# Clustered attention followed by a gated MLP on one core: routing in one matmul pass, one PV copy per period in batch 0, two items prepared later, centroid roots on GpSimd

## The chip, the core and the metric

The kernel runs on one core of a Trainium2 chip. The core's engines run side by side, each with its own queue of instructions: TensorE (PE; its weight loads are shown as PEld), VectorE (DVE), ScalarE (ACT), GpSimd (POOL) and SyncE (SP), which here only issues DMAs. The metric is the device time of one execution in microseconds (us): the median of several runs.

## What is computed

Inputs: q, k, v of 4 batches x 8 heads x 768 tokens x 64 numbers, 16 centroids per head, and two MLP weight matrices (512 x 2048 and 2048 x 512).

```python
q_n, k_n, c_n = (t / (norm(t, axis=-1) + 1e-6) for t in (q, k, centroids))
q_assign = argmax(einsum('bhsd,hcd->bhsc', q_n, c_n), axis=-1)
k_assign = argmax(einsum('bhsd,hcd->bhsc', k_n, c_n), axis=-1)
scores = q @ k.T / sqrt(64)
scores = where(q_assign == k_assign, scores, -1e9)
attn = softmax(scores) @ v
x = attn, heads side by side              # 3072 x 512
h = x @ w_in
out = (h * sigmoid(h)) @ w_out            # 3072 x 512
```

Each query attends only to the keys with the same nearest centroid; then comes an MLP whose hidden values are multiplied by their own sigmoid.

## The kernel before

**Tiles.** Tokens lie 128 to a tile; a head has 6 query tiles and 6 key tiles. q and k are split into two f16 numbers, hi and lo, so that products of 128 numbers (hi and lo of 64) give nearly f32 results. After the codes have been written over the lo half, a score is a product over 96 rows: 64 of hi and 32 of a one-hot code of the centroid.

**Items.** The routing of queries and keys is done in 34 items (line 71). Items 0 to 7 hold the 6 key tiles and the first 3 query tiles of one head of batch 0; items 8 and 9 hold the other query tiles of four heads each; items 10 to 33 hold the 12 tiles of one head of batches 1 to 3. Item n is head n - 2 from there on. For each item, in this order:

1. `load_qk` (105): DMAs on SP into a `qk` buffer (4 of them).
2. `hi` (136, ACT) and `lo` (142, DVE): the split into `hl` (3 buffers).
3. Transpose: for items 0 to 7 `pe_tr` (154, PE, into PSUM) and `tr_out` (164, copies by ACT and DVE); for items 8 to 33 `xpose` (147), a transposing DMA issued by SP into an `ab` buffer (5).
4. `logits` (174): per tile two matmuls with 16 columns, accumulated in PSUM: the tile against `stk` (the centroids' high part, twice) and against `ckl` (their low part). The sum lies in `psL`, in a PSUM buffer of the group "mm" (2 buffers) up to item 11, then of the group "pv" (1 buffer).
5. `am_max` (189, DVE): the maximum over 16 columns, read from `psL`, then a one-hot mask (`is_ge`), read from `psL` too.
6. `am_back` (197) and `codes` (204), both on DVE: the mask is transposed in 32 x 32 blocks and written in four copies of 32 rows into the item's tile.

**Attention.** The kernel issues its work in steps T (lines 536 to 564); six steps are one period p, which is one head for batches 1 to 3 (p = 8 to 31). In batch 0 a period is half of two heads: three query tiles of heads 2(p % 4) and 2(p % 4) + 1. In step T stand, in this order: the scores of step T + 1 (`qk_mm`, 215; two PSUM buffers "st"), then logits, PE transposes and `x_tr` if they are due, a part of the MLP (`pop_mlp`), `pv_mm` if due, the `exp` of step T on ACT, from T = 48 on `am_max`, the MLP's pending activations of the step before, `evac` if due, and then whatever else is due in T in the order in which it was listed.

`pv_mm` (251) multiplies the weights P with v and a column of ones, so that the last of 65 columns is the softmax's denominator; the result is `pO`, in the one PSUM buffer of the group "pv". `evac` (267, DVE) takes the reciprocal of that column and multiplies, into `xp`. In batch 0 a period has two such pairs, c = 0 and 1, one per head: `pv_mm` in steps 6p + 4 and 6p + 7, `evac` one step after each, three blocks of 64 columns at a time. From batch 1 on there is one `evac` of six blocks per period. In batch 0 and for the last two heads `x_tr` (281, PE, into "mm") transposes `xp`, and `x_out` (288, ACT) copies it to `xt`, the MLP's input; for the other heads a transposing DMA does it (`x_dma`, 296).

**MLP.** `unit_a` (309) is four matmuls of 384 columns into `ph` ("mm", 2 buffers), then tanh on ACT (320) and one operation on DVE (321) into `gt`. `unit_b` (329) is four matmuls of 512 columns into `po`, and after four of those a copy (342) and the output DMA. `pop_mlp` (350) issues units at rates fixed by the step. `ready` (510) says in which step the MLP may start on a half batch; what is left after the last step is done in the loop at 572.

**When an item's work is due.** `due(n)` (458) is d, the step in which an item must be routed: 6(n - 2) - 1 for n >= 10. For n >= 10, logits stand at d - 6, `am_max` at d - 5, `am_back` and `codes` at d - 4, `xpose` at d - 23, `lo` at d - 25, `hi` at d - 27, `load_qk` at d - 40. For items 8 and 9 `xpose` stands at d - 11. All of it is written out by hand: nothing is reordered later, and each engine's queue runs strictly in this order.

**The start** (376 to 455). SP loads the centroids, then items 0 to 2, v of head 0 and item 3. PE runs `fill(10)`, ten matmuls on zeros whose result nobody reads. ACT loads its table for square roots, squares and sums the centroids (405) and takes the root (407); DVE refines the root in two rounds of four operations (417 to 428), with `lo(0)` between them; then six operations end in `chl`, the centroids in f16 high and low parts. `fill(4)` (442) stands on PE ahead of the transpose of `chl` (444), and three copies on DVE (446 to 448) write `stk` and `ckl`. Then come `lo(1)`, `logits(0)` and so on.

Of the kernel before, what the change touches and what calls it, by code (L numbers as in the profile page):

```python
# [9 lines left out]
f32 = mybir.dt.float32  # L10
f16 = mybir.dt.float16
AF = mybir.ActivationFunctionType
ALU = mybir.AluOpType
AX = mybir.AxisListType
# [3 lines left out]
def kernel(  # L18
# [10 lines left out]
    nc = tc.nc  # L29
    B, H, S, D = q.shape  # L30
    HC = centroids.shape[1]
# [3 lines left out]
    NJ = S // 128  # L35
# [3 lines left out]
    HALF = S // 2  # L39
# [5 lines left out]
    NSPLIT = H // 2  # L45
# [4 lines left out]
    const = ctx.enter_context(tc.tile_pool(name="const", bufs=1))  # L50
# [4 lines left out]
    wout_s = const.tile([128, NFB, DM], f16, name="wout_s")  # L55
    xts = [[const.tile([128, S], f16, name=f"xt{r}_{n}") for r in range(NR)] for n in range(2)]
    vts = [const.tile([128, NJ, D + 2], f16, name=f"vt{n}") for n in range(H)]
    stk = const.tile([128, H, HC], f16, name="stk")
    ckl = const.tile([128, H, HC], f16, name="ckl")

    ohp = [[const.tile([128, 12, 32], f16, name=f"oh{m}_{n}") for n in range(r)] for m, r in enumerate((2, 1, 2))]
    mxs = const.tile([128, 34, 12], f32, name="mxs")
# [15 lines left out]
    def head_of(p, s):  # L78
        return 2 * (p % NSPLIT) + s if p < H else p
# [18 lines left out]
    def width(n):  # L98
        return 3 * len(items[n])
# [41 lines left out]
    @per_item  # L141
    def lo(n):
        ho, lw, src = parts(n)
        nc.vector.scalar_tensor_tensor(out=lw, in0=src, scalar=QS, in1=ho, op0=ALU.mult, op1=ALU.subtract)  # L144
# [9 lines left out]
    def pe_tr(n):  # L154
        hl = hls[n]
        trs[n] = []
        for a, w in ((0, NJ), (NJ, NJ // 2)):
            tag, bufs = ("po", 1) if a == 0 else ("mm", 2)
            pT = ps.tile([128, w * 128], f16, name="pT", tag=tag, bufs=bufs)
            for t in range(w):  # L160
                nc.tensor.transpose(pT[:, 128 * t : 128 * t + 128], hl[:, a + t].rearrange("p c d -> p (c d)"), ident)
            trs[n].append(pT)
# [7 lines left out]
        abs_[n] = ab  # L170


    @per_item
    def logits(n):
        ab, w = abs_[n], width(n)

        tag, bufs = ("mm", 2) if n < H + 4 else ("pv", 1)
        psL = ps.tile([128, 12, HC], f32, name="psL", tag=tag, bufs=bufs)[:, 0:w]
        for t in range(w):
            for c, st in ((stk, True), (ckl, False)):  # L180
                nc.tensor.matmul(psL[:, t, :], ab[:, t, :], c[:, items[n][t // 3][0] % H, :], start=st, stop=not st)  # L181
        psLs[n] = psL

    def oh_of(n):
# [3 lines left out]
    @per_item  # L188
    def am_max(n):
        psL, w = psLs.pop(n), width(n)  # L190
        mx = mxs[:, n, 0:w]
        nc.vector.tensor_reduce(out=mx, in_=psL, axis=AX.X, op=ALU.max)
        nc.vector.tensor_tensor(
            out=oh_of(n)[:, :, 0:HC], in0=psL, in1=mx.unsqueeze(2).to_broadcast([128, w, HC]), op=ALU.is_ge
        )
# [53 lines left out]


    def pv_mm(p, c, i0, i1):
        hd = head_of(p, c)
        if i0 == 0:
            pOs[p, c] = ps.tile([128, NJ, D + 2], f32, name="pO", tag="pv", bufs=1)
        for i in range(i0, i1):
            for j in range(NJ):
                if p < H:
                    o = (j % 2) * HALF + 128 * i
                    lhsT = Ps[NJ * p + 3 * c + j // 2][:, o : o + 128]
                else:  # L260
                    lhsT = Ps[NJ * p + j][:, 128 * i : 128 * i + 128]
                nc.tensor.matmul(  # L262
                    pOs[p, c][:, i, 0 : D + 1], lhsT, vts[hd % H][:, j, 0 : D + 1], start=(j == 0), stop=(j == NJ - 1)
                )


    def evac(p, c):
        hd, pO = head_of(p, c), pOs.pop((p, c))
        i0, w = (3 * (p // NSPLIT), 3) if p < H else (0, NJ)
        if hd % 2 == 0:  # L270
            xps[hd // 2] = mp.tile([128, NJ, 128], f16, name="xp", bufs=3)
        xp = xps[hd // 2]
        rz = rzs[:, hd, i0 : i0 + w]
        nc.vector.reciprocal(rz, pO[:, 0:w, D])
        nc.vector.tensor_tensor(  # L275
            out=xp[:, 0:w, D * (hd % 2) : D * (hd % 2) + D], in0=pO[:, 0:w, 0:D],
            in1=rz.unsqueeze(2).to_broadcast([128, w, D]), op=ALU.mult,
        )


# [7 lines left out]
    def x_out(hd, a, w):  # L288
        b, r = divmod(hd // 2, NR)
        for i in range(w // 3):  # L290
            o = 128 * a + i * HALF
            nc.scalar.activation(
                out=xts[b % 2][r][:, o : o + HALF], in_=pXs.pop((hd // 2, i)), func=AF.Copy, bias=0.0, scale=1.0
            )

    def x_dma(hd):
        b, r = divmod(hd // 2, NR)
# [59 lines left out]
    def fill(n):  # L357
        if n:
            junk = ps.tile([128, 1024], f32, name="junk", tag="st", bufs=2)[:, 0:512]
            for _ in range(n):  # L360
                nc.tensor.matmul(junk, zz[:, 0:128], zz, start=True, stop=True)  # L361
# [13 lines left out]

    nc.vector.memset(zz, 0.0)
    cw_ = mp.tile([128, D], f32, name="craw")
    nc.sync.dma_start(cw_, centroids.rearrange("h c d -> (h c) d"))
    load_qk(0)
    load_qk(1)  # L380
    load_qk(2)
# [4 lines left out]
    def at(T, f, *a):  # L386
        steps.setdefault(T, []).append((f, a))

    nc.scalar.preload_act_table(AF.Sqrt)
    fill(10)  # L390
    ident = const.tile([128, 128], f16, name="ident")
    make_identity(nc, ident)
# [8 lines left out]
    abks = [g0[:, 1152 * n : 1152 * (n + 1)].rearrange("p (n c) -> p n c", c=128) for n in range(5)]  # L401
    abks += [const.tile([128, 9, 128], f16, name=f"abk{n}") for n in range(5, H)]
    csq = mp.tile([128, D], f32, name="csq")
    cs = mp.tile([128, 1], f32, name="cs")
    nc.scalar.activation(out=csq, in_=cw_, func=AF.Square, bias=0.0, scale=1.0, accum_out=cs)
    cy = mp.tile([128, 1], f32, name="cy", bufs=3)
    nc.scalar.activation(out=cy, in_=cs, func=AF.Sqrt, bias=0.0, scale=1.0)
    hi(0)
    nc.scalar.preload_act_table(AF.Exp)
    for vt in vts:  # L410
        nc.gpsimd.memset(vt[:, :, D : D + 2], 1.0)
    for oh in ohp[1] + ohp[2]:
# [1 line left out]
        nc.gpsimd.memset(oh[:, :, HC : HC + 1], 1.0)  # L414
    for oh in ohp[2]:
        nc.gpsimd.memset(oh[:, 0:NJ, HC : HC + 1], -1.0)
    for i in range(2):
        cr = mp.tile([128, 1], f32, name="cr", bufs=2)
        nc.vector.reciprocal(cr, cy)
        ct = mp.tile([128, 1], f32, name="ct", bufs=2)  # L420
        nc.vector.tensor_tensor(out=ct, in0=cs, in1=cr, op=ALU.mult)
        ct2 = mp.tile([128, 1], f32, name="ct2", bufs=2)
        nc.vector.tensor_tensor(out=ct2, in0=ct, in1=cy, op=ALU.add)
        cy = mp.tile([128, 1], f32, name="cy", bufs=3)
        nc.vector.tensor_scalar(out=cy, in0=ct2, scalar1=0.5, scalar2=None, op0=ALU.mult)
        if i == 0:
            lo(0)
            pe_tr(0)
    cyp = mp.tile([128, 1], f32, name="cyp")
    nc.vector.tensor_scalar(out=cyp, in0=cy, scalar1=1e-6, scalar2=None, op0=ALU.add)  # L430
    cinv = mp.tile([128, 1], f32, name="cinv")
# [7 lines left out]
    )  # L439
    tr_out(0)  # L440
    hi(1)
    fill(4)
    pst1 = ps.tile([128, 128], f16, name="pst1", tag="mm", bufs=2)
    nc.tensor.transpose(pst1, chl.rearrange("p a d -> p (a d)"), ident)
    chv = pst1[0:64, :].rearrange("d (h c) -> d h c", c=HC)
    nc.vector.tensor_copy(stk[0:64], chv)
    nc.vector.tensor_copy(stk[64:128], chv)
    nc.vector.tensor_copy(ckl[0:64], pst1[64:128, :].rearrange("d (h c) -> d h c", c=HC))
    lo(1)
    logits(0)  # L450
    pe_tr(1)
# [13 lines left out]
    for n in range(NI):  # L465
        d = due(n)
        near = n < H + 2
        if n < H:
            if n > 0:
                at(3 * n - 3, am_back, n)  # L470
                at(3 * n - 3, codes, n)
                at(3 * n - 4, am_max, n)
                at(3 * n - 5, logits, n)
            if n > 1:
                at(3 * n - 8, tr_out, n)
                at(3 * n - 9, pe_tr, n)
                at(3 * n - 11, lo, n)
                at(3 * n - 12, hi, n)
        else:
            e = d + 2 if near else d  # L480
            at(e - 4, am_back, n)
            at(e - 4, codes, n)
            at(e - 5, am_max, n)
            at(e - 6, logits, n)
            x = d - (11 if near else 23)
            at(x, xpose, n)
            at(x - 2, lo, n)
            at(x - 4, hi, n)
        if n > 3:
            at(d - (24 if near else 40), load_qk, n)  # L490
    for n in range(NBH):
        hd = n
# [18 lines left out]
    for p in range(NBH):  # L511
        if p < H:
            for c in range(2):
                T = NJ * p + 3 * c + 4
                pv_at[T] = (p, c, 0, 3)
                evac_at[T + 1] = (p, c)
            E = T + 1
            at(E + 1, x_tr, 2 * (p % NSPLIT), 3, "mm")
            at(E + 1, x_out, 2 * (p % NSPLIT), 3 * (p // NSPLIT), 3)
            if p % NSPLIT == NSPLIT - 1:  # L520
                ready[E + 3] = [(0, p // NSPLIT)]
            continue
        T = NJ * (p + 1) + 1
        for i in range(3):
            pv_at[T + i] = (p, 0, 2 * i, 2 * i + 2)
        E = T + 3
        evac_at[E] = (p, 0)
        if p == NBH - 1:
            at(E + 1, x_tr, p - 1, NJ, "mm")
            at(E + 1, x_out, p - 1, 0, NJ)  # L530
        elif p % 2 == 1:
            at(E + 1, x_dma, p - 1)
            if p % H == H - 1:
                ready[E + 8] = [(p // H, 0), (p // H, 1)]
# [76 lines left out]
```

## Time and profile before

| | |
|---|---|
| median of 3 runs | 339.13 us (338.73 to 339.54) |
| the profiled execution | 339.54 us |
| its span in the profile | 337.8 us |
| PE busy | 314.1 us (93%) |
| ACT busy | 235.5 us (70%) |
| DVE busy | 220.0 us (65%) |
| POOL busy | 33.8 us (10%) |
| chain that ended last: PE, DVE, ACT, DMA | 70%, 11%, 7%, 7% |

The profile shows one execution: when each instruction started and ended, and what an idle engine waited for. Matmuls are pipelined: each lasts longer than the distance to the next one's start, so many short ones add up to more busy time than they take of the queue. A group is named by line, engine and tiles (out<-in), with partitions x elements, the count, the busy time, the mean of one, and the idle time ahead of its instructions with who ended it. Batch 0's periods run from about 12 to 84 us, those of batches 1 to 3 until some 270 us, and after that only the MLP is left. The granted clock is the share of full speed at which TensorE's clock ran.

### The profile page before, as it was taken

The page shows a single profiled execution, that of the slowest core. Times are in us where ns is not written, and L with a number is a line of the kernel's source. Part 1 is how long each engine was busy: PE and PEld are TensorE (multiplying, and loading weights), DVE is VectorE, ACT ScalarE, POOL GpSimd, SP SyncE. Part 2 cuts the span into 40 slices and gives each one's busy share as a digit, 9 for nine tenths or more (in the row PEclk, how much of TensorE's full clock was granted, in tenths as well). Part 3 has the DMA queues.
Part 4 walks back from the last instruction along what each step waited for, and adds up shares of the span by engine and source line. Part 5 has one row for each costly group of instructions (what it writes and reads, how often), then busy time and mean ns, then how long its engine had stood idle before and what let it go on. Part 6 is the DMA issues. An engine that isn't in the chain of part 4 may idle for free.

```text
span 337.8 us, 8356 instructions
## 1 busy us (share of the span) xinstructions
PE 314.1 (93%) x3350; PEld 190.8 (57%) x3350; DVE 220.0 (65%) x537; ACT 235.5 (70%) x377; POOL 33.8 (10%) x84
## 2 busy tenths in 40 slices
PE   7787978967999999999998999999999999999995
PEld 3455645644666665566665666666666654555542
DVE  5899774675877768756777777766655442365431
ACT  6797898968988888787788777877778541264310
POOL 3234222130000000100000000000000000000000
PEclk9997999999999999999999999999999999999999
DMA  6799999985577676897296666362301001100121
GB/s 187 191 229 206 221 127 231 177 173 126 123 174 165 167 187 171 151 236 129 99 191 148 120 165 145 88 102 65 79 33 25 31 33 54 73 0 0 37 88 63
DMA packets 71510, 42.32 MB, mean 125 GB/s; under 512 B 52016, under 2 KB 67376, under 8 KB 71472
## 3 DMA queue, kind: packets, MB, share of 16 engines
q1 hardware_dynamic: 68144, 37.60, 47.1%
q0 software_dynamic: 3328, 4.20, 8.0%
q8 instruction: 26, 0.43, 0.5%
q14 instruction: 12, 0.10, 0.1%
HBM read 27.30 MB, written 6.29 MB: 99 GB/s over the span
## 4 chain that ended last, share of the span: by engine, by line
PE 70%; DVE 11%; ACT 7%; DMA 7%; issue 3%; SPq 1%; DVEq 0%; ACTq 0%
PE po L335 23%; PE ph L316 16%; PE pS L231 7%; PE pO L262 7%; PE psL L181 5%; PE sth L316 4%; PE pS L232 4%; DMA qk<-in_q_dram 3%; DVE gt L321 3%; DMA ab<-hl 2%; ACT P L246 2%; ACT tn L320 2%; ACT P L241 2%; PE junk L361 2%; DVE hl L144 2%
## 5 line engine op out<-in xcount | busy, mean ns | idle before, releaser
L246 ACT ACTIVATE P<-pS 128x768 f16<-128x768 f32 x144 | 114.5, 816 | 29.7 <-PE pS L232 28.6
L321 DVE SCALAR_TENSOR_TENSOR gt<-tn,ph 128x384 f16<-128x384 f32 x105 | 58.0, 553 | 58.4 <-ACT tn L320 57.1
L335 PE MATMUL po<-wout_s,gt 128*128 128x512 f16 x384 | 94.3, 379 | 0.0
L316 PE MATMUL ph<-xt,win_s 128*128 128x384 f16 x420 | 84.6, 325 | 2.1 <-DVE gt L321 1.8
L316 PEld LDWEIGHTS <-win_s 128*128 128x128 f16 x512 | 48.4, 97 | 36.4 <-issue 3.1
L320 ACT ACTIVATE tn<-ph 128x384 f32<-128x384 f32 x105 | 52.0, 495 | 16.8 <-PE ph L316 15.6
L335 PEld LDWEIGHTS <-gt 128*128 128x128 f16 x384 | 37.0, 97 | 37.4
L262 PEld LDWEIGHTS <-P 128*128 128x128 f16 x1152 | 47.4, 97 | 14.3 <-DVE xp L275 0.8
L231 PE MATMUL pS<-ab 96*128 96x512 f16 x144 | 54.3, 380 | 1.1 <-ACT P L246 1.1
L262 PE MATMUL pO<-vt,P 128*128 128x65 f16 x1152 | 50.8, 193 | 0.5 <-DVE xp L275 0.4
L241 ACT ACTIVATE P<-pS 128x768 f16<-128x768 f32 x48 | 37.9, 813 | 5.3 <-PE pS L225 5.0
L232 PE MATMUL pS<-ab 96*128 96x256 f16 x144 | 38.9, 270 | 0.0
L127 POOL CAST vt<-vn 128x384 f16<-128x384 f32 x32 | 18.4, 574 | 174.2 <-DMA vn<-in_v_dram 110.5
L144 DVE SCALAR_TENSOR_TENSOR hl<-qk,hl 128x768 f16<-128x768 f32 (+1 forms) x34 | 30.8, 911 | 1.0 <-ACT hl L139 0.8
L320 ACT ACTIVATE tn<-sth 128x384 f32<-128x384 f32 x23 | 11.0, 490 | 27.2 <-PE sth L316 20.1
L207 DVE TENSOR_SCALAR ab<-ohT 32x384 f16<-32x384 f16 x104 | 27.5, 264 | 1.9
L139 ACT ACTIVATE hl<-qk 128x768 f16<-128x768 f32 (+1 forms) x34 | 27.3, 808 | 1.3 <-DMA qk<-in_q_dram 1.3
L342 DVE TENSOR_SCALAR ot<-po 128x512 f32<-128x512 f32 x24 | 16.5, 688 | 17.7 <-PE po L335 17.2
L181 PEld LDWEIGHTS <-ab 128*128 128x128 f16 x624 | 18.7, 96 | 8.6 <-issue 5.3
L321 DVE SCALAR_TENSOR_TENSOR gt<-tn,sth 128x384 f16<-128x384 f32 x23 | 12.5, 553 | 14.1 <-ACT tn L320 14.1
L181 PE MATMUL psL<-stk,ab 128*128 128x16 f16 x312 | 18.8, 169 | 3.0 <-DVE xp L275 1.8
L275 DVE TENSOR_TENSOR xp<-pO,rzs 128x384 f16<-128x384 f32 (+1 forms) x40 | 19.1, 477 | 1.4
(73 smaller groups left out, 248.1 us busy)
## 6 DMA issues: line engine op xcount, KB each, us to landing
qk<-in_k_dram SPq DMA_DIRECT2D x32, 192.0 KB, 3.3
vn<-in_v_dram SPq DMA_DIRECT2D x32, 192.0 KB, 3.3
out_dram<-ot SPq DMA_DIRECT2D x24, 256.0 KB, 2.0
qk<-in_q_dram SPq DMA_DIRECT2D x24, 192.0 KB, 3.1
win_s<-in_moe_w_in_dram POOLq DMA_DIRECT2D x8, 256.0 KB, 6.1
wout_s<-in_moe_w_out_dram POOLq DMA_DIRECT2D x8, 256.0 KB, 6.0
qk<-in_q_dram SPq DMA_DIRECT2D x16, 96.0 KB, 4.0
ab<-hl SPq DMA_TRANSPOSE x26, 3.9
```

The lines of the kernel that those rows point to most:

```text
L144: nc.vector.scalar_tensor_tensor(out=lw, in0=src, scalar=QS, in1=ho, op0=ALU.mult, op1=ALU.subtract)
L181: nc.tensor.matmul(psL[:, t, :], ab[:, t, :], c[:, items[n][t // 3][0] % H, :], start=st, stop=not st)
L207: nc.vector.tensor_scalar(out=ab[64:96, 0:w, 32 * g : 32 * g + 32], in0=ohT[32 * g : 32 * g + 32, :].rearrange("p (t i) -> p t i", i=32), ...
L231: nc.tensor.matmul(pS[:, 0:512], lhsT, q_tiles(p, 0, 4), start=True, stop=True)
L232: nc.tensor.matmul(pS[:, 512:768], lhsT, q_tiles(p, 4, 2), start=True, stop=True)
L241: nc.scalar.activation(out=P.rearrange("p (c x) -> p c x", c=2), in_=pS.rearrange("p (c x) -> p c x", c=2)[:, :, 0:HALF], func=AF.Exp, bia ...
L246: nc.scalar.activation(out=P, in_=pS[:, 0:S], func=AF.Exp, bias=0.0, scale=ESC)
L262: nc.tensor.matmul(pOs[p, c][:, i, 0 : D + 1], lhsT, vts[hd % H][:, j, 0 : D + 1], start=(j == 0), stop=(j == NJ - 1))
L316: nc.tensor.matmul(ph, win_s[:, r, ts(fb, 128)], xts[b % 2][r][:, T0 : T0 + HALF], start=(r == 0), stop=(r == NR - 1))
L320: nc.scalar.activation(out=tn, in_=ph, func=AF.Tanh, bias=0.0, scale=0.5)
L321: nc.vector.scalar_tensor_tensor(out=gt[:, fb, :], in0=tn, scalar=1.0, in1=ph, op0=ALU.add, op1=ALU.mult)
L335: nc.tensor.matmul(po, gt[:, fc, ts(t, 128)], wout_s[:, fc, :], start=(fc == 0), stop=(fc == NFB - 1))
```

## The change

1. **Routing.** `stk` and `ckl` become the two halves of one tile `cst`, 32 columns per head. For items 10 to 33 `logits` issues one matmul of 32 columns per tile instead of two of 16, and `psL` has 32 columns per tile: both parts side by side. `am_max` first sums the two halves with a reduction on DVE into `lg`, in SBUF; maximum and mask read `lg`. Items 0 to 9 stay with two matmuls.
2. **Batch 0's PV.** Both pairs of a period share one `pO` (three blocks each); one `evac` per period, at step 6p + 8, divides all six.
3. **Batch 0's transposed output.** For p >= 4, `x_tr` and `x_out` come two steps after `evac` instead of one, with `ready` following, and `x_out` is a copy on DVE, after the other work listed for that step (`lo` of a later item among it), instead of one on ACT.
4. **Items 10 and 11.** `xpose`, `lo` and `hi` stand at d - 15, d - 17 and d - 19: eight steps later. The DMA of item 12 (step 36) then stands ahead of that of item 11 (step 38) on SP.
5. **The start.** The centroid DMA goes to ACT's queue. ACT loads only the table of exp. Square and sum are two operations on DVE; the root is one operation on GpSimd, a power of 0.5, behind a memset; the two refining rounds are gone. `fill(4)` ahead of the transpose of `chl` becomes `fill(3)` behind it.

The loads (`load_qk`), the rates of the MLP and the work after the last step are the same.

```diff
-    stk = const.tile([128, H, HC], f16, name="stk")
-    ckl = const.tile([128, H, HC], f16, name="ckl")
+    cst = const.tile([128, H, 2 * HC], f16, name="cst")
+    stk, ckl = cst[:, :, 0:HC], cst[:, :, HC : 2 * HC]
...
     def logits(n):
-        psL = ps.tile([128, 12, HC], f32, name="psL", tag=tag, bufs=bufs)[:, 0:w]
+        two = n < H + 2
+        psL = ps.tile([128, 12, HC if two else 2 * HC], f32, name="psL", tag=tag, bufs=bufs)[:, 0:w]
         for t in range(w):
-            for c, st in ((stk, True), (ckl, False)):
-                nc.tensor.matmul(psL[:, t, :], ab[:, t, :], c[:, items[n][t // 3][0] % H, :], start=st, stop=not st)
+            hd = items[n][t // 3][0] % H
+            if two:
+                for c, st in ((stk, True), (ckl, False)):
+                    nc.tensor.matmul(psL[:, t, :], ab[:, t, :], c[:, hd, :], start=st, stop=not st)
+            else:
+                nc.tensor.matmul(psL[:, t, :], ab[:, t, :], cst[:, hd, :], start=True, stop=True)
...
     def am_max(n):
+        if n >= H + 2:
+            lg = mp.tile([128, 12, HC], f32, name="lg", bufs=2)
+            nc.vector.tensor_reduce(out=lg, in_=psL.rearrange("p t (s c) -> p t c s", s=2), axis=AX.X, op=ALU.add)
+            psL = lg
...
     def pv_mm(p, c, i0, i1):
-        if i0 == 0:
-            pOs[p, c] = ps.tile([128, NJ, D + 2], f32, name="pO", tag="pv", bufs=1)
+        if i0 == 0 and c == 0:
+            pOs[p] = ps.tile([128, NJ, D + 2], f32, name="pO", tag="pv", bufs=1)
...
-    def evac(p, c):
+    def evac(p):
+        if p < H:
+            i0 = 3 * (p // NSPLIT)
+            rz = rzs[:, hd : hd + 2, i0 : i0 + 3]
+            nc.vector.reciprocal(rz, pO[:, :, D].rearrange("p (c t) -> p c t", c=2))
+            nc.vector.tensor_tensor(
+                out=xp[:, 0:3, :].rearrange("p t (c d) -> p c t d", c=2),
+                in0=pO[:, :, 0:D].rearrange("p (c t) d -> p c t d", c=2),
+                in1=rz.unsqueeze(3).to_broadcast([128, 2, 3, D]), op=ALU.mult,
+            )
+            return
...
     def x_out(hd, a, w):
+            if b == 0 and a > 0:
+                nc.vector.tensor_copy(dst, src)
+            else:
+                nc.scalar.activation(out=dst, in_=src, func=AF.Copy, bias=0.0, scale=1.0)
...
-    nc.sync.dma_start(cw_, centroids.rearrange("h c d -> (h c) d"))
+    nc.scalar.dma_start(cw_, centroids.rearrange("h c d -> (h c) d"))
...
-    nc.scalar.preload_act_table(AF.Sqrt)
+    nc.scalar.preload_act_table(AF.Exp)
...
-    nc.scalar.activation(out=csq, in_=cw_, func=AF.Square, bias=0.0, scale=1.0, accum_out=cs)
-    nc.scalar.activation(out=cy, in_=cs, func=AF.Sqrt, bias=0.0, scale=1.0)
+    nc.vector.tensor_tensor(out=csq, in0=cw_, in1=cw_, op=ALU.mult)
+    nc.vector.tensor_reduce(out=cs, in_=csq, axis=AX.X, op=ALU.add)
+    nc.gpsimd.memset(half, 0.5)
+    nc.gpsimd.tensor_tensor(out=cy, in0=cs, in1=half, op=ALU.pow)
...
-    nc.scalar.preload_act_table(AF.Exp)
...
-    for i in range(2):
-        nc.vector.reciprocal(cr, cy)
-        nc.vector.tensor_tensor(out=ct, in0=cs, in1=cr, op=ALU.mult)
-        nc.vector.tensor_tensor(out=ct2, in0=ct, in1=cy, op=ALU.add)
-        nc.vector.tensor_scalar(out=cy, in0=ct2, scalar1=0.5, scalar2=None, op0=ALU.mult)
...
-    fill(4)
     nc.tensor.transpose(pst1, chl.rearrange("p a d -> p (a d)"), ident)
...
+    fill(3)
     lo(1)
...
-            x = d - (11 if near else 23)
+            x = d - (11 if near else 15 if n < H + 4 else 23)
...
-                evac_at[T + 1] = (p, c)
             E = T + 1
-            at(E + 1, x_tr, 2 * (p % NSPLIT), 3, "mm")
-            at(E + 1, x_out, 2 * (p % NSPLIT), 3 * (p // NSPLIT), 3)
+            evac_at[E] = (p,)
+            X = E + (1 if p < NSPLIT else 2)
+            at(X, x_tr, 2 * (p % NSPLIT), 3, "mm")
+            at(X, x_out, 2 * (p % NSPLIT), 3 * (p // NSPLIT), 3)
             if p % NSPLIT == NSPLIT - 1:
-                ready[E + 3] = [(0, p // NSPLIT)]
+                ready[X + 2] = [(0, p // NSPLIT)]
```

## The prediction

> **What bounds the kernel now.** I read busy times first, then stages, then who waits for whom, then the chain and the timeline.
>
> Part 1 and two rows of part 2 of the page:
>
> ```profile
> PE 314.1 (93%) x3350; PEld 190.8 (57%) x3350; DVE 220.0 (65%) x537; ACT 235.5 (70%) x377; POOL 33.8 (10%) x84
> ...
> DVE  5899774675877768756777777766655442365431
> ...
> PEclk9997999999999999999999999999999999999999
> ```
>
> An average of several stages, so next the busy times by stage (after the bounds: length, then busy us of PE, PEld, DVE, ACT, POOL):
>
> ```profile
> 10.00:36.00 26.00, 21.21 (x291) 13.63 (x290) 22.75 (x64) 21.32 (x31) 8.64 (x19) 0.93 0.97 217
> 36.00:84.00 48.00, 39.17 (x500) 25.11 (x498) 32.30 (x84) 41.14 (x67) 10.19 (x21) 1.00 0.93 176
> 84.00:130.00 46.00, 45.25 (x576) 29.44 (x575) 34.79 (x83) 39.89 (x63) 3.38 (x6) 1.00 0.64 154
> 130.00:190.00 60.00, 57.45 (x714) 36.50 (x712) 43.66 (x104) 48.88 (x77) 4.03 (x8) 1.00 0.72 161
> 190.00:255.00 65.00, 64.89 (x742) 40.98 (x739) 44.05 (x106) 49.65 (x78) 3.29 (x6) 1.00 0.46 97
> ```
>
> From 84 us PE lacks 0.75, 2.55 and 0.11 us of being always busy: PE bounds there. In 36 to 84 us it stands idle 8.8 us of 48; in 10 to 36 us VectorE is the fullest (22.75 of 26). Who makes PE wait, in 36 to 84 us and in 84 to 190 us (waiter, releaser: total, times, longest):
>
> ```profile
> PE pX L285 <- DVE xp L275: 3.5, 3, 1.7
> ...
> PE pS L225 <- ACT P L241: 1.9, 5, 0.7
> ...
> PE ph L316 <- DVE gt L321: 1.5, 3, 0.5
> ...
> PE psL L181 <- DMA ab<-hl: 0.8, 1, 0.8
> ```
>
> ```profile
> PE psL L181 <- DVE xp L275: 1.8, 3, 0.9
> ...
> PE pS L231 <- ACT P L246: 1.1, 4, 0.3
> ```
>
> The costs of routing are in the groups kept apart by shape:
>
> ```profile
> L181 PE MATMUL psL<-stk,ab 128*128 128x16 f16 x312 | 18.8, 169 | 3.0 <-DVE xp L275 1.8 <-DMA ab<-hl 0.8
> ...
> L193 DVE TENSOR_TENSOR oh<-psL,mxs 128x192 f16<-128x192 f32 x26 | 9.3, 357 | 1.0
> L192 DVE TENSOR_REDUCE mxs<-psL 128x12 f32<-128x192 f32 x26 | 9.2, 353 | 4.5 <-PE psL L181 4.3
> ```
>
> A mean of 169 ns is the length of one pipelined matmul, not its price; that is the spacing of starts. In the timeline at 198.47 us 24 of them start from 198.47 to 199.04 us, and PE goes on at 199.07: 0.60 us, 25 ns each.
>
> The profiled execution took 339.54 us (span 337.8, 1.7 around it), 0.4 above the median 339.13. I work on its span and take the sum off the median. A run of this kernel can tell about 0.2% (0.7 us) from no change.
>
> **1. Routing in one pass of 32 columns (items 10 to 33).** Removed: 12 of 24 matmuls for 24 items. If a 32-column matmul also starts every 25 ns, PE gives up 12 x 25 = 0.30 us per item. Rows on both sides: 16 columns 25 ns; 65 columns (pO, 12 in 0.54 us of which the last takes 0.193) (0.54-0.193)/11 = 31.5 ns. With 31.5 the item costs 0.38 instead of 0.60 and 0.22 is saved. I take 0.30, as 32 lies nearer to 16; 0.22 stays for the range. The Trainium skill (TensorE: Matmul & The Clock Gate, Back-to-back issue gap) says the same for a stronger reason: up to 64 columns the spacing is a floor of some 25 ns; by it the saving is 0.30 and 0.22 is out, and the 25 ns of the trace agree for 16 columns.
>
> Added: 24 sums on VectorE, 384 f32 from PSUM. Not in the trace; the nearest row is gt L321, 384 f32 from PSUM, at 553 ns, and 353 ns for 192 (max) is the lower end. A pair is a short row, and the max, with 12 rows of 16, costs the same as the elementwise 357, so rows have been free: I take 0.55. Max and mask then read SBUF; I leave them at 0.35. VectorE gains 24 x 0.55 = 13 us. What hides it: it is idle 11.2, 16.3 and 21.0 us in the three stages from 84 us, some 2.2, 2.4 and 2.9 us in each 8.9 us period. Behind the sum in its queue stand max, mask and the gt of the unit issued in the step before. In the timeline (199.25 to 200.44 us) gt stood 0.44 us after the mask waiting for tanh. The sum starts 0.30 earlier and the mask ends 0.25 later: still inside 0.44. psL's buffer, which PV wants at 201.88, is now free after the sum (about 199.3) instead of the mask (200.0).
>
> How much of PE's 0.30 arrives: 7 items lie in 190 to 255 us, where PE never waits: 2.1 us. 15 lie in 84 to 190 us: 4.5 us, but the chain runs by ACT, DVE and a DMA in two stretches, 122 to 147 and 165 to 181 us, some 40 of 106 us, and nothing arrives there: 2.8, less 0.3 where the sum lies on the chain. Items 10 and 11 lie where PE is not the bound: 0. **Term: -4.6** (0 to -6.6).
>
> **2. One PV copy per period in batch 0.** 16 pairs of 0.176+0.357 = 0.53 become 8 of 0.192+0.557 = 0.75 (the rows for six blocks): VectorE -2.5 us over batch 0. In the stage that it bounds (10 to 36 us) the copies of steps 5, 8, 11 (1.6 us) become that of step 8 (0.75): **-0.9** (0 to -2.6: the granted clock fell to 0.7 in slice 4 after PE had waited 1.5 us for VectorE at 29.06 us; over 26 us at 0.93 that cost 1.7 us, which go too if PE stays busy enough).
>
> **3. 36 to 84 us.** x_tr of p >= 4 comes a step after the copy instead of in it, so PE's 3.5 us for xp go; what is late next is the exp on ACT (1.9), which loses four copies of 0.49 us to VectorE, and gt (1.5). The four copies stand on VectorE behind lo (0.95 us) and hold one of two mm buffers as long, so the next but one ph can wait: about 0.5 each, 2 us given back at worst. Items 10 and 11: hi, lo and the transposing DMA move 8 steps. Their DMA is no longer behind that of item 9, whose landing took 7.8 us against a median of 3.9 and cost PE the 0.8 (longer on the chain). Behind them on SP nothing waits for long: the load of item 14 waits for lo of item 10, one step before; the DMA of item 12 now precedes 11's, which has 9 steps (13 us) until its logits. Of 4.3 us that go (3.5+0.8) I keep 2.5: **-2.5** (+0.5 to -5).
>
> **4. Start.** Centroid DMA on ACT's queue: SP issues item 0's load 0.46 us earlier. That does not move PE, as the ten junk matmuls run to 5.64 us and the transposes behind them. What moves: fill(4) (0.86 us on the chain, 6.41 to 7.27) no longer stands ahead of the centroid transpose, whose operand comes at about 6.1 (lo(0) ends at 4.97, then the five operations that now take 1.13) instead of 7.24. Then the copy of 0.36 and three of 0.25 end at 7.55, but lo(1) needs hi(1), which ACT ends at 7.66 as now: the chain is 8.42 instead of 8.93, **-0.5**. GpSimd's power is in no row; POOL's copy of one column takes 0.27 us, and nothing bounds it above. It starts at about 3.0 us and is free up to 2.2 us, as lo(0) stands ahead of its reader; from 2.7 us it is a loss of 1 us per us. I take it as hidden; the memsets behind it on POOL end at about 6 us, the first cast is at 8.24.
>
> The tail from 255 us has the same work: 0.
>
> **Sum:** -4.6 -0.9 -2.5 -0.5 = -8.5. 339.1 - 8.5 = **330.6 us**.
>
> **Rivals.**
> - *VectorE takes over what PE gives (18%).* The copies behind lo return the 2.5 of part 3 as waits of ph, the sums close VectorE's gaps in the chain's two mixed stretches and before, so that only the seven items after 190 us count: 2.1 + 0.5 = 2.6 us, 336.5. For it: gt already makes ph wait (1.5). Against: VectorE waits for tanh 9.9 us in 36 to 84 us and 21.0 us in 84 to 190.
> - *All of it arrives (7%).* 6.6 + 2.6 + 4 + 0.5 = 13.7: 325.4. It needs ACT to keep pace: 39.89 of 46 us now; the shorter stage would have it at 90%.
> - *The sum is slow (9%, the slower side).* A reduction over pairs has 192 rows; if each row costs a start, one instruction takes r, not 0.55. VectorE has 2.2 us free per period from 84 us; from r = 2.2 the period grows, and from r = 2.6 (0.4 x 22 = 8.8 us) all that is won is gone. At r = 3: 22 x 0.8 = 18 us longer, less 3.9 from the other parts: 353. Against: 12 rows cost nothing visible.
> - *Nothing to be seen (6%).* The gains of PE meet a loss of like size at the start (a power of some 10 us): within 338.4 to 339.8.
>
> The forecast itself has 60%, from 327.5 to 334.5. The range 327 to 337 takes in it and most of the first rival. Faster 0.85 (60+18+7), same 0.06, slower 0.09.
>
> **What would show it.** psL starts 25 ns apart, 12 per item, 0.30 in all; the sum at 0.55 on VectorE; PE still without waits after 190 us, and periods there of 8.6 instead of 8.9 us; pX no longer waiting for xp, ph for gt not over 2 us more; the landing of item 9's transpose near 4 us; the first max at 8.4 instead of 8.96 us. I am wrong if the sum takes over 1 us, if the period after 190 us stays at 8.9, or if ph's waits for gt and xt eat what pX gave.

## The result, and the profile after

After: 337.04 us, median of 20 runs (334.34 to 339.96). Before, beside it: 339.51 us (20 runs). Ratio 0.993 (0.9909 to 0.995): 2.5 us faster, where 8.5 were forecast. Ratios, here and below, leave out runs over 1.5% above their kernel's fastest, and the median of w_xsfill leaves out one of 449 us. The profiled execution after took 338.56 us, its span is 336.8 us.

Part 1 and two rows of part 2 of the page after:

```profile
PE 309.9 (92%) x3061; PEld 185.0 (55%) x3061; DVE 231.7 (69%) x543; ACT 231.6 (69%) x369; POOL 34.1 (10%) x86
...
DVE  5898745568898888786888888777765442365431
...
PEclk9997999797999999999999999999999999999999
```

PE lost 4.2 us of work, DVE took 11.7, as wanted. But the granted clock now falls in three slices instead of one. The stages, with the same bounds as before:

```profile
10.00:36.00 26.00, 21.40 (x295) 13.84 (x294) 22.35 (x60) 21.65 (x33) 8.14 (x20) 0.93 1.02 212
36.00:84.00 48.00, 37.71 (x437) 23.70 (x436) 30.32 (x69) 35.06 (x55) 8.88 (x20) 0.93 0.88 167
84.00:130.00 46.00, 44.72 (x507) 28.34 (x505) 39.18 (x95) 41.82 (x66) 3.42 (x6) 1.00 0.72 160
130.00:190.00 60.00, 56.67 (x629) 34.99 (x630) 48.61 (x115) 50.54 (x79) 5.42 (x8) 1.00 0.75 163
190.00:255.00 65.00, 64.69 (x671) 39.96 (x670) 49.81 (x119) 50.42 (x81) 3.81 (x7) 1.00 0.49 98
```

In 36 to 84 us PE and ACT are less busy than before (37.71 for 39.17, 35.06 for 41.14) and the clock is 0.93 for 1.00: less was done in the same time (of the 6.08 us that ACT lacks, the four copies given to DVE are 2.0). Who made PE wait there:

```profile
PE ph L337 <- DVE gt L342: 4.1, 3, 2.6
PE pX L304 <- DVE xp L287: 2.1, 1, 2.1
...
PE psL L186 <- DMA ab<-hl: 0.7, 1, 0.7
```

The wait of pX for xp fell from 3.5 to 2.1; that of ph for gt rose from 1.5 to 4.1.

To see where time goes I compare starts of the same instruction, after less before. From the copy of period 8 (89.68 us before) to that of period 31 the difference runs from +4.16 to -1.01: 5.2 us won. At the mask transposes of items in batch 0 it is -0.21 (item 0), -1.13 (item 5), +0.06 (item 9, 57 us), +4.24 (item 10), +4.84 (item 11): over 4 us lost between 57 and 84 us. The first of the two places there, from the timeline: the kernel before, then DVE and PE of the kernel after.

```profile
56.33 0.34 PE L285 MATMUL pX<-ident,xp 128*128 128x128 f16 x3
56.70 0.49 ACT L292 ACTIVATE xt<-pX 128x384 f16<-128x384 f16 x1
...
56.98 0.82 PE L316 MATMUL ph<-xt,win_s 128*128 128x384 f16 x4 [0.31 <-DVE oh L193]
...
57.97 0.81 PE L316 MATMUL ph<-xt,win_s 128*128 128x384 f16 x4
...
58.80 0.56 DVE L321 SCALAR_TENSOR_TENSOR gt<-tn,ph 128x384 f16<-128x384 f32 x1
```

```profile
55.77 0.56 DVE L287 TENSOR_TENSOR xp<-pO,rzs 128x384 f16<-128x384 f32 x1
56.24 0.35 DVE L203 TENSOR_REDUCE mxs<-psL 128x12 f32<-128x192 f32 x1
56.62 0.36 DVE L204 TENSOR_TENSOR oh<-psL,mxs 128x192 f16<-128x192 f32 x1
57.02 0.58 DVE L211 STREAM_TRANSPOSE ohT<-oh 128x384 f16<-128x384 f16 x1
57.63 1.71 DVE L218 TENSOR_SCALAR ab<-ohT 32x384 f16<-32x384 f16 x4
59.37 0.55 DVE L342 SCALAR_TENSOR_TENSOR gt<-tn,ph 128x384 f16<-128x384 f32 x1
59.84 0.95 DVE L145 SCALAR_TENSOR_TENSOR hl<-qk,hl 128x768 f16<-128x768 f32 x1
60.70 0.35 DVE L313 COPY xt<-pX 128x384 f16<-128x384 f16 x1
```

```profile
56.01 0.81 PE L337 MATMUL ph<-xt,win_s 128*128 128x384 f16 x4
56.66 0.49 PE L236 MATMUL pS<-ab,gt 96*128 96x384 f16 x2
57.03 0.33 PE L304 MATMUL pX<-ident,xp 128*128 128x128 f16 x3
59.97 1.44 PE L337 MATMUL ph<-xt,win_s 128*128 128x384 f16 x4 [2.61 <-DVE gt L342]
61.20 1.20 PE L273 MATMUL pO<-vt,P 128*128 128x65 f16 x18
```

In the kernel before, pX stands ahead of both ph, ACT empties it at once, and the second ph (57.97) starts before the first one's gt. In the kernel after, pX comes in step 34: it takes one mm buffer (57.03), and a ph of the step before holds the other until its gt, which stands on DVE behind the copy of six blocks and the whole routing of item 9. PE is idle for 2.61 us. Then its own work is slow: ph takes 1.44 us instead of 0.81, pO 1.20 instead of 0.73. The second place is at 79 us: pX waits 2.08 us for xp, behind the codes of item 10.

### The profile page after: what moved, and what is told of

Read it like the earlier page. It is cut to its first block, busy times and chain, and to the rows that moved or that the text cites. A ratio compares the mean times of both kernels' runs of the same rounds, so it can differ in the third digit from the quotient of the medians.

```text
span 336.8 us, 7761 instructions
## 1 busy us (share of the span) xinstructions
PE 309.9 (92%) x3061; PEld 185.0 (55%) x3061; DVE 231.7 (69%) x543; ACT 231.6 (69%) x369; POOL 34.1 (10%) x86
## 4 chain that ended last, share of the span: by engine, by line
PE 67%; DVE 15%; ACT 6%; DMA 6%; issue 3%; SPq 1%; DVEq 0%; ACTq 0%
PE po L356 23%; PE ph L337 17%; PE pO L273 7%; PE pS L242 7%; PE sth L337 4%; PE pS L243 4%; DVE gt L342 3%; DVE hl L145 3%; ACT P L257 2%; DMA ab<-hl 2%; DMA vn<-in_v_dram 2%; ACT tn L341 2%; PE psL L188 2%; DVE ab L218 2%; DMA qk<-in_q_dram 2%
## 5 line engine op out<-in xcount | busy, mean ns | idle before, releaser
L337 PE MATMUL ph<-xt,win_s 128*128 128x384 f16 x420 | 85.8, 328 | 5.2 <-DVE gt L342 5.0
L273 PEld LDWEIGHTS <-P 128*128 128x128 f16 x1152 | 48.3, 98 | 13.9 <-DVE lg L200 0.4
L273 PE MATMUL pO<-vt,P 128*128 128x65 f16 x1152 | 51.5, 195 | 0.0
L218 DVE TENSOR_SCALAR ab<-ohT 32x384 f16<-32x384 f16 x104 | 28.2, 271 | 2.0
L211 DVE STREAM_TRANSPOSE ohT<-oh 128x384 f16<-128x384 f16 (+1 forms) x34 | 18.7, 550 | 0.7
L243 PEld LDWEIGHTS <-ab 96*128 96x128 f16 x144 | 14.3, 99 | 7.8 <-issue 2.9
L242 PEld LDWEIGHTS <-ab 96*128 96x128 f16 x144 | 14.2, 98 | 6.5 <-issue 0.4
```

The lines of the kernel that those rows point to most:

```text
L218: nc.vector.tensor_scalar(out=ab[64:96, 0:w, 32 * g : 32 * g + 32], in0=ohT[32 * g : 32 * g + 32, :].rearrange("p (t i) -> p t i", i=32), ...
L242: nc.tensor.matmul(pS[:, 0:512], lhsT, q_tiles(p, 0, 4), start=True, stop=True)
L243: nc.tensor.matmul(pS[:, 512:768], lhsT, q_tiles(p, 4, 2), start=True, stop=True)
L273: nc.tensor.matmul(pOs[p][:, o3 + i, 0 : D + 1], lhsT, vts[hd % H][:, j, 0 : D + 1], start=(j == 0), stop=(j == NJ - 1))
L337: nc.tensor.matmul(ph, win_s[:, r, ts(fb, 128)], xts[b % 2][r][:, T0 : T0 + HALF], start=(r == 0), stop=(r == NR - 1))
```

## The experiments

Three theories. **T1:** the later step of `x_tr` is the loss, as pX and ph meet in the two mm buffers while gt is late. **T2:** the copy out of pX on DVE is, as the first rival had it. **T3:** the half clock behind each wait is a price of its own. Each kernel ran beside the kernel before on the same chip (medians of before 339.4 to 339.7 us; the sets ran on different chips); clock: the median over the runs of a kernel, four to twenty of each.

| kernel | median us | ratio to before | clock |
|---|---|---|---|
| after | 337.04 | 0.993 (0.991 to 0.995) | 0.985 |
| a_xact | 336.16 | 0.988 (0.985 to 0.992) | 0.990 |
| a_xstep | 336.55 | 0.991 (0.988 to 0.994) | 0.990 |
| a_p3undone | 335.70 | 0.989 (0.987 to 0.991) | 0.994 |
| b_route | 335.24 | 0.988 (0.985 to 0.991) | 0.994 |
| a_fill | 335.31 | 0.988 (0.985 to 0.991) | 0.994 |
| u_items | 335.18 | 0.989 (0.987 to 0.991) | 0.994 |
| u_pv2 | 334.61 | 0.986 (0.984 to 0.988) | 0.995 |
| u_craw | 336.65 | 0.993 (0.990 to 0.995) | 0.990 |
| b_fill | 338.46 | 0.997 (0.996 to 0.999) | 1.000 |
| v_fill | 334.10 | 0.986 (0.982 to 0.989) | 0.994 |
| v_two | 332.69 | 0.981 (0.979 to 0.984) | 1.000 |
| a_pv2 | 335.66 | 0.990 (0.987 to 0.993) | 0.988 |
| w_p3 | 334.69 | 0.986 (0.983 to 0.989) | 0.995 |
| w_p3fill | 333.29 | 0.984 (0.981 to 0.987) | 1.000 |
| w_xsfill | 333.48 | 0.982 (0.980 to 0.984) | 1.000 |

**Which move (a_xact, a_xstep, a_p3undone).**

```diff
a_xact, a_p3undone:
-            if b == 0 and a > 0:
-                nc.vector.tensor_copy(dst, src)
-            else:
+            if True:
                 nc.scalar.activation(out=dst, in_=src, func=AF.Copy, bias=0.0, scale=1.0)
a_xstep, a_p3undone:
-            X = E + (1 if p < NSPLIT else 2)
+            X = E + 1
```

> The kernel after, with the six x_out copies that the change puts on VectorE in batch 0 given back to ScalarE; x_tr keeps its new step. Measured so far: the kernel after is 2.5 us ahead of the one before, 5.2 us were won after 90 us, and 4 to 5 us were lost between 57 and 84 us. T1 (the new step of x_tr makes pX share the two mm buffers with ph, while gt stands behind the copy of six blocks and the codes on VectorE): nothing changes, 336 to 338 us, and PE still waits 2 us and more at ph for gt near 60 us. T2 (the copy out of pX on VectorE holds the buffer, as rival 1 had it): the loss goes, 332.5 to 333.5 us, and no wait of PE over 1 us is left between 55 and 84 us. T3 (the price is doubled by the clock, which falls after each wait of PE over 2 us) goes with either: where a wait stays, the granted clock of 60-70 us stays near 0.83; where it goes, the clock is 0.95 or more.

> The kernel after, with x_tr a step after the copy throughout (X = E + 1), as in the kernel before; the copies out of pX stay on VectorE. T1 (the new step is the cause): the loss of 4 to 5 us between 57 and 84 us goes but for PE's own waits pX for xp, 332.5 to 334 us, the clock of 60-70 us back at 0.95 or more. T2 (the copy out on VectorE is the cause): 336 to 338 us; PE waits over 2 us at ph near 58 us, then for the copy out of pX.

> The kernel after with both of these given back: x_tr a step after the copy, all copies out of pX on ScalarE. What is left of the change is the routing in one pass, one PV copy per period, items 10 and 11 eight steps later, and the start. T1 and T2 both say the loss between 57 and 84 us goes: 332.5 to 334 us (339.5 less 5.2 for the routing, less 0.7 for the PV copies, less 0.2 for the start). Against both, a third: if the loss is that of the items moved later or of the single PV copy, the time stays at 336 to 338 us.

Neither T1 nor T2 is the cause alone: each move undone by itself left 336.2 and 336.6 us, with intervals that overlap that of the kernel after; both undone gave 335.7, between the two forecasts. The change puts four copies on DVE, not six. The wait near 58 us becomes shorter (2.61 to 1.41 and 1.59), stays and changes its releaser, first in the timeline of a_xact, then in that of a_xstep:

```profile
57.53 0.81 PE L335 MATMUL ph<-xt,win_s 128*128 128x384 f16 x4 [1.41 <-ACT xt L313]
```

```profile
58.97 0.81 PE L337 MATMUL ph<-xt,win_s 128*128 128x384 f16 x4 [1.59 <-DVE xt L313]
```

The copy out waits on ACT behind `hi` or on DVE behind the codes. And both undone is 1.1 us short of 334.6 (u_pv2, below): part of the loss lies in another part of the change.

**The routing alone (b_route):** the kernel before with the diff's `cst`, `logits` and `am_max`.

> The kernel before, with the routing in one pass of 32 columns and its sum on VectorE from item 10 on, and nothing else of the change. If the 0.30 us per item that the trace of the kernel after shows from the ninth period on belongs to this part alone: 339.5 less 5.2 to 6.5, so 333.0 to 334.5 us. If the sum of items 10 and 11 on VectorE is itself what delays gt between 70 and 84 us: 335.5 us or more, with a wait of PE for gt there.

335.24 us, so -4.45: between the two. From period 8 to 31 the difference to before runs from +0.50 to -4.92. The loss ahead of it comes with items 10 and 11: -0.30 at the exp of step 45 (71.9 us), +0.49 at step 54 (84.8 us), as PE waits there for DVE. In 36 to 84 us, b_route (before: 3.5 and 1.5):

```profile
PE pX L294 <- DVE xp L284: 4.3, 3, 2.3
PE ph L325 <- DVE gt L330: 2.1, 3, 0.8
```

**The clock (a_fill, b_fill).**

```diff
a_fill, ahead of x_tr in step 46 and behind it in step 34:
-        if i0 == 0 and c == 0:
+        if i0 == 0 and c == 0 and p != 5:
...
+        if T == 46:
+            for _ in range(30):
+                nc.tensor.matmul(pst[47][:, 896:1024], zz[:, 0:128], zz[:, 0:128], start=True, stop=True)
...
+        if T == 34:
+            pOs[5] = ps.tile([128, NJ, D + 2], f32, name="pO", tag="pv", bufs=1)
+            for _ in range(12):
+                nc.tensor.matmul(pOs[5].rearrange("p n d -> p (n d)"), zz[:, 0:128], zz[:, 0:396], start=True, stop=True)
b_fill:
-            if T < 40 and T % 3 != 2:
+            for _ in range(4 if T == 11 else 1 if T < 40 and T % 3 != 2 else 0):
                 nc.tensor.matmul(pS[:, 0:512], zz[:, 0:128], zz, start=True, stop=True)
```

> The kernel after, with idle matmuls on zeros (nothing reads them) put on TensorE into two of its waits: 12 of 128x396 between pX and ph of step 34, and 30 of 128x128 ahead of pX of step 46, some 2 us of work at each place. No wait gets shorter; TensorE only looks busy. T3 (most of what the kernel after loses against the one with part 3 undone, 337.0 to 335.7 us, is the half clock that a wait in a 3.4 us interval brings on in the next; over the runs so far each such interval goes with about 1.2 us): the intervals at half clock near 60 and 80 us go, the mean clock rises from 0.984 to 0.99 or more, and the time falls to 334.5 to 335.5 us, with the same waits of DVE. Against it, the waits themselves are the whole loss: 336.5 to 338 us, whatever the clock does.

> The kernel before with four idle matmuls of 128x512 on zeros ahead of the scores of step 11, where TensorE waits some 1.2 to 1.5 us at 28 us; nothing reads them. If the half clock at 28 to 31 us comes of that wait in the 3.4 us interval ahead of it (T3): the interval goes, clock 1.000, and 338.0 to 338.6 us, 1.2 us less. If it has another reason: no change, 339.0 to 340 us.

T3 held in both. The same place in the timeline of a_fill; the wait is as long, but filled, and the work behind it runs at full speed:

```profile
56.43 0.33 PE L304 MATMUL pX<-ident,xp 128*128 128x128 f16 x3
56.59 2.17 PE L567 MATMUL pO<-zz 128*128 128x396 f16 x12
59.37 0.81 PE L337 MATMUL ph<-xt,win_s 128*128 128x384 f16 x4 [0.61 <-DVE gt L342]
60.02 0.73 PE L273 MATMUL pO<-vt,P 128*128 128x65 f16 x18
```

In the trace's record the clock stands at 0.5 for 3.41 us at a time (more on this at the end). The stretches of that length with the wait and behind it, after and then a_fill (length, busy us as above; the last three columns: granted clock, DMA share, GB/s):

```profile
56.51:59.93 3.42, 0.85 (x7) 0.48 (x6) 3.24 (x9) 2.53 (x5) 2.21 (x5) 1.00 0.40 61
59.93:63.34 3.41, 3.37 (x26) 2.08 (x26) 2.50 (x4) 0.49 (x1) 0.00 (x0) 0.50 1.01 133
```

```profile
55.62:59.04 3.42, 3.15 (x21) 1.77 (x20) 3.24 (x9) 2.82 (x5) 2.22 (x5) 1.00 0.39 70
59.04:62.45 3.41, 3.08 (x33) 2.02 (x33) 2.84 (x5) 1.61 (x3) 0.00 (x0) 1.00 1.09 146
```

Behind a stretch with PE busy 0.85 of 3.42 us the clock is 0.50; behind one with 3.15 it stays at 1.00. a_fill gave 1.7 us back (337.04 to 335.31, in two sets of runs); b_fill 1.0 for the one interval that the kernel before has, from 29.9 us (ratio 0.9973, 0.996 to 0.9985).

**What else was lost (u_items, u_pv2, u_craw),** each on top of a_p3undone:

```diff
u_items:
-            x = d - (11 if near else 15 if n < H + 4 else 23)
+            x = d - (11 if near else 23)
u_pv2: pv_mm, evac and evac_at as in the kernel before
u_craw:
-    nc.scalar.dma_start(cw_, centroids.rearrange("h c d -> (h c) d"))
+    nc.sync.dma_start(cw_, centroids.rearrange("h c d -> (h c) d"))
```

> The kernel with part 3's two moves undone (335.7 us), and items 10 and 11 put back to 23 steps ahead as in the kernel before. The exp of step 52 stood 1.45 us later there than in the kernel before, and 0.50 us later in the one with the routing alone; 0.95 us are lost between steps 33 and 52 to the single PV copy, the later items or the start. If the later items are that loss: step 52 at +0.3 to +0.6 and 334.5 to 335.0 us. If the single PV copy is: no change, 335.5 to 336 us.

> The kernel with part 3's two moves undone (335.7 us), and two PV copies per period in batch 0 as in the kernel before; items 10 and 11 stay later. If the single copy (six blocks in one go, behind which the codes of an item wait, and which comes only after the second PV) is what gives back 0.95 us between steps 24 and 52: step 52 at +0.3 to +0.6 against the kernel before, and 334.5 to 335.0 us, though the 0.5 us that it won up to step 15 are gone too. If the later items are: 335.5 to 336.5 us.

> The kernel with part 3's two moves undone (335.7 us), and the centroids' load back on SyncE's queue, so that they land near 2.5 us and not 3.6 us. If that landing is why the start gained 0.2 to 0.4 us and not 0.5 us: the transposes of item 0 at -0.8 to -1.3 us against the kernel before (-0.44 with the load on ScalarE), and 0.3 to 0.8 us less at step 8; by the end it may be lost again. If the slow VectorE instructions on the centroids (0.48 us for 0.25, beside GpSimd's memsets) are: -0.4 to -0.6 us. In the time: 334.8 to 335.7 us, too little to tell apart but by the trace.

u_pv2: the single copy costs 1.1 us (0.8 by the ratios, whose intervals overlap); the starts in the two profiles say where. The exp of step 6, 15, 24, 33 and 48 stands at -0.43, -0.79, -0.36, -0.12 and +1.23 us against before with the single copy, at -0.62, -1.18, -1.18, -1.44 and -0.75 with two; step 52, expected at +0.3 to +0.6, is at -0.53. So by step 15 it had won nothing that two copies had not (0.36 against 0.56 from step 6), and from then on it loses: in step 20 the copy of six blocks (0.75 us for 0.53) stands ahead of item 8's maximum, which starts at 41.16 us, with two copies at 40.34. u_items: 335.18, 0.5 less, between the two forecasts and its interval on top of a_p3undone's; step 52 at +0.5, where the first expectation had it. Both cannot be the whole of one loss: u_pv2 has the later items too, and is ahead. u_craw: 336.65, outside its forecast; the load on SP lands 1.1 us sooner, and the start wins nothing more (-0.27 at item 0), as item 0's load is now behind it on SP: `lo(0)` starts at 5.13 us, in u_pv2 at 4.58; of the rest, one wait of 1.15 us for item 8's DMA and two intervals at half clock, I settled nothing.

**The best of it (v_fill, v_two),** and part 3 again without the single copy (a_pv2: the kernel after with pv_mm, evac and evac_at as before). v_fill is u_pv2 with b_fill's edit; v_two is v_fill with:

```diff
-        two = n < H + 2
+        two = n < H + 4
...
-        if n >= H + 2:
+        if n >= H + 4:
             lg = mp.tile([128, 12, HC], f32, name="lg", bufs=2)
```

> The best so far (the change with part 3's moves undone and two PV copies per period: 334.6 us) with the same four idle matmuls at step 11. T3: no interval at half clock is left, 333.2 to 333.8 us. Without T3: 334.4 to 335 us.

> As the one with four idle matmuls at step 11, and items 10 and 11 with their routing in two passes as in the kernel before: one pass only from item 12 on. The routing alone was 0.3 us ahead of the kernel before up to step 45 and 0.5 us behind at step 52. If the 0.55 us sum of those two items on VectorE, on which TensorE waits there, is that loss: step 52 some 0.6 to 0.8 us earlier than in its neighbour, and 332.6 to 333.2 us. If not: the same as its neighbour, 333.2 to 333.8 us.

> The kernel after with two PV copies per period in batch 0 again; part 3 stays whole (x_tr a step later, its copies out on VectorE, items 10 and 11 later). Beside the same kernel without part 3's two moves (334.6 us) it gives part 3 by itself. The prediction had part 3 at -2.5 us: 332 us. If part 3 is a loss of its own by its waits and the clock: 335.5 to 336.5 us, with an interval at half clock after 55 us. If it loses only together with the copy of six blocks: 334 to 335 us and no such interval.

v_two is the fastest: 332.69 us, 6.8 less than before, 4.3 less than after. Its exp stands at -1.70 in step 45 and in step 54, where u_pv2 went from -1.33 to -0.53: the sum of two items cost 0.8 us, as in b_route. v_fill came out 0.5 below u_pv2, inside the scatter and between its two forecasts; its profile shows a half clock elsewhere, behind a wait of 2.27 us at 73.55 us, which v_two does not have. Waits of v_two in 36 to 84 us; its clock is 1.00 throughout:

```profile
PE pX L296 <- DVE xp L286: 3.5, 3, 1.7
PE ph L327 <- DVE gt L332: 1.5, 3, 0.5
```

These are the waits of the kernel before, to the tenth. a_pv2 at 335.66 is 1.05 slower than u_pv2, as the second forecast had it, with an interval at half clock from 59.3 us: part 3 loses by itself.

**Part 3 with the clock held up (w_p3, w_p3fill, w_xsfill):** v_two with part 3's two moves back; the same with a_fill's idle matmuls; and that with the copies out on ACT.

> The fastest kernel so far (v_two: 332.69 us, clock 1.000 in most runs) with part 3's two moves put back: x_tr of p >= 4 two steps after the copy, its copies out on VectorE. If they lose by waits and clock as in the pair of a_pv2 and u_pv2: 334 to 336 us, with an interval at half clock after 55 us in most runs and a mean clock of 0.990 to 0.995. As the prediction had part 3: 330.2 us.

> The same with idle matmuls on zeros in the two waits (12 of 128x396 between pX and ph of step 34, 30 of 128x128 ahead of pX of step 46), so that the clock stays up: mean clock 0.998 or more. What is left is part 3's waits alone. If these win what the prediction had less the price of the clock: 330 to 331 us. If the waits for gt eat what pX gave (as the total of TensorE's waits for VectorE in 36 to 84 us has it: 6.2 us with the moves, 7.1 without): 332.0 to 333.2 us, no difference to v_two. If they lose by themselves: 333.5 us or more.

> As w_p3fill, with the copies out of pX on ScalarE: the later x_tr alone. If the copy on VectorE, behind lo and the codes, holds the buffer that ph wants: 0.5 to 1 us faster than w_p3fill. If gt behind the codes is the whole wait: the same within 0.4 us. If ScalarE's own queue (exp, hi, tanh) holds the copy as long: the same, with ph waiting for xt from ScalarE.

With the moves 334.69, filled 333.29 (just between its last two forecasts), without the moves 332.69. Taking only runs at clock 0.998 or more, w_p3 has 333.4 and 333.5, w_p3fill 333.0 to 333.3, v_two 332.3 to 333.0: by these few runs the waits alone cost 0.6 to 0.8 us, which is near the scatter, and the rest of the 2.0 is the clock. In w_p3fill the idle matmuls cover pX's wait for xp, and of the wait of ph near 58 us 0.43 is left behind 2.17 us of them: some 2.6 us, as long as in the kernel after. w_xsfill is the same within 0.3 us; its only profile is that of the 449 us, so who holds ph there is not seen.

## Why the prediction was wrong, step by step

**1. Routing, -4.6: right in sum.** b_route measured -4.45. psL starts of the profile after, 12 in 0.46 us of which the last takes 0.177: 25.7 ns each; the next item is 8.59 us later, as forecast (8.6).

```profile
199.17 0.46 PE L188 MATMUL psL<-cst,ab 128*128 128x32 f16 x12
```

```profile
L200 DVE TENSOR_REDUCE lg<-psL 128x192 f32<-128x384 f32 x24 | 13.3, 553 | 2.6 <-PE psL L188 2.4
...
L204 DVE TENSOR_TENSOR oh<-lg,mxs 128x192 f16<-128x192 f32 x24 | 8.9, 372 | 0.9
L203 DVE TENSOR_REDUCE mxs<-lg 128x12 f32<-128x192 f32 x24 | 8.5, 353 | 0.8
```

The sum costs the 0.55 us forecast. Two errors cancel: of the stretches in which "nothing arrives", 122 to 147 us gave the full 0.30 per period (+2.97 to +1.76 from period 12 to 16), and only behind 172 us nothing came for a while (+0.86 to +1.00 from period 19 to 21); and items 10 and 11, put at 0, cost 0.8. That the sum fits is luck.

**2. One PV copy, -0.9: wrong in sign, +1.1** (u_pv2). I costed the stage that DVE bounds, 10 to 36 us, where it won nothing, and not what stands behind the longer, later copy in the stage after: the routing of an item, and gt. The gain from the clock that stood in its range did not come either: the interval at half clock near 29 us stayed, in the kernel after and in u_pv2.

**3. 36 to 84 us, -2.5: the step that failed.** The two moves cost 1.3 us (a_p3undone), 1.05 (a_pv2) and 2.0 (w_p3) in three settings: a loss each time, though the intervals of each pair touch, so that the size is rough. 3.8 of the 6.0 us that the forecast missed are here, 2.0 in part 2. "PE's 3.5 us for xp go" was half true (3.5 to 2.1); what took their place I had named, ph on an mm buffer, but at "2 us given back at worst" and for the wrong reason: I put the four copies behind `lo`, while ph waited for gt, which stood on DVE behind the copy, maximum, mask and codes of the two steps before. And for these 48 us neither term nor rival had the clock as a price: waits that had been three of up to 1.7 us became one of 2.6 and one of 2.1, and each brought an interval at half clock, 1.7 us together (a_fill). The landing of item 9's DMA took 7.9 us as before with item 10's no longer behind it, and PE's wait was 0.7 instead of 0.8: that reason was wrong too. Moving the items did no harm by itself: v_two, which has them, stands at -1.81 in step 33 and -1.70 in step 54. But in the profiles of all twelve kernels with the later items (w_xsfill left out, as everywhere below) the four writes of item 9's codes (L218) take 1.70 to 1.72 us, and 1.14 to 1.19 in the four with the items as before (before, b_route, b_fill, u_items). So some 0.5 of the 2.61 us came with the moved items; why the writes are slower is open.

**4. Start, -0.5: right on the mean.** The profile after shows -0.21 at item 0; the profiles of the eleven other kernels with that start -0.25 to -0.79, the mean of all twelve is -0.45. The centroids on ACT's queue land 2.8 us after issue (1.7 on SP before); the power is hidden.

Taken in one order, from the kernel before over b_route, u_pv2 and a_p3undone to the kernel after, the medians give -4.45 for the routing, -0.6 for start and later items, +1.1 for the copy, +1.3 for part 3's two moves: -2.65. Steps in a row add up to the whole (-2.5) whatever each of them is, but for the sets of runs; this says where the time went, not that the terms are independent (part 3 costs 1.05 with two copies and 2.0 on top of v_two). The first rival, 336.5 us, was nearest in time and had the right place; its mechanism (the copies behind `lo`, and sums that take back part 1) was not the one.

## What to carry to other kernels

A wait that is moved is costed with what stands in the releaser's queue in the new step, not with its old length; list that queue in order. For the clock, not the sum of the waits counts but how little PE does in any 3.41 us: three waits of up to 1.7 us in 36 to 84 us left it alone, one of 2.61 and one of 2.08 did not, and one of 1.49 us near 29 us, where PE was only 0.46 busy, did not either. Idle matmuls in such a place are worth more than they look (1.0 to 1.7 us here). A gain on the engine that bounds is paid for by work on another only where that other has slack: the same edit won 0.30 us per item after 90 us and lost 0.4 per item before.

## What the hardware showed beside

**The clock.** In the trace's own record it falls to 0.5 for 3.41 us at a time: in the profile after, from 29.2, 59.9 and 80.4 us of the span, and the ph of 59.97 us is the first slow one of the second. The distances, 30.7 and 20.5 us, are 9 and 6 times 3.41, so the intervals lie on a grid, and each execution has its own (the first is at 29.9 us before, at 28.3 in a_fill). What the traces tie them to is how busy PE was in the stretch of the grid just ahead: 0.46, 0.25 and 0.39 of it here. In the sixteen profiles all 17 intervals between 10 and 320 us came behind a stretch with PE busy 0.61 or less; all ten stretches at 0.46 or less were followed by one, and 7 of the 24 between 0.47 and 0.61. So whether a wait costs an interval depends on where it falls: 2.61 and 2.08 us did here; one of 2.48 us in a_p3undone, up to 75.53 us, lay across two stretches of the grid and did not. Runs of one kernel differ with it: after's three runs at a clock near 0.995 average 335.3 us, its ten near 0.985 337.8. The Trainium skill (TensorE: Matmul & The Clock Gate, What's actually happening) describes a free-running window of 3413 ns after which the clock is halved or restored, and the traces agree with its 3.41 us. It puts the half rate behind an idle window; here no window was idle throughout, as the busy shares show.

**DVE beside GpSimd's memsets.** In the start of the profile after, two DVE operations on 64 columns take twice their time just while a memset of 384 columns runs on POOL (0.25 and 0.20 in the kernel before, and in u_craw, where the same memsets have ended before):

```profile
5.60 0.48 DVE L447 TENSOR_SCALAR cn<-craw,cinv 128x64 f32<-128x64 f32 x1
6.12 0.49 DVE L449 TENSOR_SCALAR chl<-cn 128x64 f16<-128x64 f32 x1
```

```profile
5.61 0.42 POOL L436 MEMSET oh<- 128x384 f16 x1
...
6.13 0.42 POOL L436 MEMSET oh<- 128x384 f16 x1
```

The Trainium skill (GPSIMD Engine Reference, Specifications) has GpSimd share its SBUF interfaces with VectorE, with contention where VectorE's instruction runs in a 2-port mode or reads two inputs from SBUF; the pairs above agree with contention, though no run here shows which mode these two operations ran in. The power on one column takes 0.57 us on GpSimd (L431, at 4.23 us). Maximum and mask are no cheaper from SBUF (353 and 372 ns) than from PSUM (353 and 357).
